# Transposing the rows of the second LayerNorm in blocks 0 to 2 with VectorE instead of TensorE

## The chip, the core and the metric

The kernel runs on one core of a Trainium2 chip. The core has five engines that each take their instructions in program order: TensorE (PE in the profile, with its weight loads shown apart as PEld), VectorE (DVE), ScalarE (ACT), GpSimd (POOL) and SyncE (SP), which here only issues DMAs. They wait for each other through semaphores. The metric is the device time of one launch in microseconds, the median of several runs.

## What is computed

One transformer block on 2048 rows of 512 elements, in float32: an attention with 32 heads of 16 that share one key and one value head, then a gated feed-forward layer with 1792 hidden elements.

```python
x = A_x
h = x + attention(layernorm(x), wq, wk, wv, wo)        # 32 heads, one k and one v
h2 = h + (gelu(layernorm(h) @ w_gate) * (layernorm(h) @ w_up)) @ w_down
return h2
```

The change concerns `layernorm(h)`, the second LayerNorm. Its rows must be turned, so that the 512 model elements stand on the partitions, before the products with `w_gate` and `w_up` can be taken.

## The kernel before

The 2048 rows are worked on in four blocks of 512, each of four tiles of 128 rows (`t` 0 to 3). Attention runs through all blocks as one long stream of scores: for each group of four heads and each chunk of 128 keys, TensorE makes two pairs of score tiles (`s`, L371), ScalarE takes the exponential of each pair (`p`, L375), and TensorE later weighs the values with them (`acc`, L379). One `s` move is a pair of matmuls and one exponential over 128x1024 elements.

The dense work of blocks 0 to 2 is woven into the attention of the blocks after them. It is a queue of products, made in this order for block `b`: four projections `pp_b_t` (the attention output times `wo`), two remaining products `pd` of block `b-1` with `w_down`, then `pg` and `pu` for each of the 14 chunks of the hidden elements (gate and up), with `pd` in between. All terms are split in a high and a low part, so a projection has 12 terms. Each product is made twice, on the upper and on the lower 64 rows of the array (`pp_b_t_0` and `pp_b_t_1` in the order of instructions), in two PSUM banks; VectorE adds both into an SBUF tile. One `d` move (`step`, L808) issues one matmul of the first half and, six moves behind (`LAG`), one of the second, which run beside each other. The halves take the three spare banks in turn, first in, first out.

The order of the stream is written out by hand. `CYCLES` (L47) lists rounds of `s` and `d` moves; each round begins with `finish`, which issues the value weighings of two or three chunks. A round is called idle when the queue cannot give enough `d` moves (`available`, L767): it then uses a second list with `s` and `v` (weighing) alone. A product may carry a condition; `pg_b_0`, the first of the gate products, may be started only when all four tiles of its block have been turned.

At the end of each half product and at the start of each round the program issues up to two steps of a side queue, `later` (`side`, L577). VectorE's and SyncE's instructions are in the order in which the program issues them, and no scheduler moves them; the same holds for TensorE, ScalarE and GpSimd.

For tile `t` the way from projection to turned rows is: `done` (L609 to L615) adds the two halves into `h`; `norm` takes mean and variance on VectorE (`bn_stats`, `bn_aggr`) and lets GpSimd make `rstd`; the step `scale` lets VectorE write the normalised rows over the input tile `xb` (L603). `before`, at the start of a round, calls `turn` once `SETTLE` = 14 moves have passed since then: four TensorE transposes into a spare PSUM bank (`pxt`, L624), from which VectorE makes the high part `x2h` (L629) and the low part `x2l` (L630). `turn` also issues the load of the input tile three ahead (`load_x`, L551); the pool `xb` has three buffers. The variable `clock` counts program moves, not time.

Of the kernel before, what the change touches and what calls it, by code (L numbers as in the profile page):

```python
# [9 lines left out]
F32 = mybir.dt.float32  # L10
# [4 lines left out]
ALU = mybir.AluOpType  # L15
# [4 lines left out]
P = 128  # L20
# [21 lines left out]

LAG = 6

SETTLE = 14

CYCLES = (  # L47
    (3, "ssdddddsdddsddds", "vssvssvs"),
# [11 lines left out]
def kernel(  # L60
# [12 lines left out]
    nc = tc.nc  # L73
    x = x.flatten_outer_dims()
# [8 lines left out]
    TB = T // P  # L83
    DC = D // P
# [19 lines left out]
    ident = const.tile([P, P], F32, name="ident")  # L104
# [54 lines left out]
    def run(outer, first):  # L159
# [304 lines left out]
        db = tiny = None  # L464
# [86 lines left out]
        def load_x(i):  # L551
            b, t = divmod(i, TB)
            if b == NB - 1:
                return
            xbs[b, t] = db.tile([P, D], F32, tag="xb", bufs=3, name=f"xb_{b}_{t}")
            nc.sync.dma_start(xbs[b, t], x_t[:, i, :])

        w1s, w2s, xbs, hs, xTs = {}, {}, {}, {}, {}
        scaled_at, halves, gs, gated = {}, {}, {}, set()
        tanhs, later = [], []  # L560
        clock = 0

        def new_xT(b):
            xTs[b] = [
                db.tile([P, DC, T], F32R, tag=f"x2{w[0]}", bufs=1, name=f"x2{w[0]}_{b}")
                for w in ("hi", "lo")
            ]

        def prime():
            new_xT(0)  # L570
            for i in range(3):
                load_x(i)
                load_w1(i)
            for j in range(3):
                load_w2(0, j)
# [13 lines left out]
        def project(b, t):  # L589
            def terms():  # L590
                o_hi, o_lo = o_blk[b]
                sl = slice(t * P, (t + 1) * P)
                return product_terms([
                    (None, (o_hi[:, c, sl], o_lo[:, c, sl]), (wo_hi[:, c, :], wo_lo[:, c, :]))
                    for c in range(DC)
                ])

            def norm():
                x = xbs[b, t]
                scaled = layer_norm(tiny, x, hs[b, t], f"2_{b}_{t}")  # L600

                def scale():
                    scaled()  # L603
                    scaled_at[b, t] = clock

                later.insert(min(1, len(later)), scale)

            def done(a, bank):
                if a == 0:  # L609
                    h = db.tile([P, D], F32, tag="h", bufs=6, name=f"h_{b}_{t}")  # L610
                    nc.vector.tensor_tensor(h, bank, xbs[b, t], op=ALU.add)
                    hs[b, t] = h
                else:
                    nc.vector.tensor_tensor(hs[b, t], hs[b, t], bank, op=ALU.add)
                    later.append(norm)  # L615

            return f"pp_{b}_{t}", 3 * DC, terms, done, lambda: pieces.get(b, 0) > t

        def turn(b, t):
            tag, bank = take_bank(f"pxt_{b}_{t}")  # L620
            pt = bank.rearrange("p (c q) -> p c q", c=DC)
            xn = xbs.pop((b, t))
            for c in range(DC):
                nc.tensor.transpose(pt[:, c, :], xn[:, c * P : (c + 1) * P], ident)  # L624
            if b not in xTs:
                new_xT(b)
            sl = slice(t * P, (t + 1) * P)
            hi, lo = (x[:, :, sl] for x in xTs[b])
            nc.vector.tensor_copy(hi, pt)  # L629
            nc.vector.tensor_tensor(lo, pt, hi.bitcast(F32), op=ALU.subtract)  # L630
            spare.append(tag)
            load_x(b * TB + t + 3)
            turned[b] = t + 1

        turned = {}

        def up(b, f, k):
            def terms():
                w = w1s.pop((b, f, k))
                hi, lo = xTs[b]  # L640
                return product_terms([
                    (None, (w[:, 0, c, :], w[:, 1, c, :]), (hi[:, c, :], lo[:, c, :]))
                    for c in range(DC)
                ])
# [12 lines left out]
            def done(a, bank):  # L657
                tag = "gu"[k]
                if a == 0:
                    half = db.tile([P, T], F32, tag=tag, bufs=2, name=f"{tag}_{b}_{f}")  # L660
                    nc.vector.tensor_copy(half, bank)  # L661
                    halves[b, f, k] = half
                else:
                    half = halves[b, f, k]
                    nc.vector.tensor_tensor(half, half, bank, op=ALU.add)  # L665
                    load_w1(b * 2 * FC + 2 * f + k + 3)
                    if k == 0:
                        later.extend((square, cube))
                    else:
                        later.append(lambda: tanhs.append((b, f)))  # L670

            ready = (lambda: turned.get(b, 0) == TB) if f == 0 and k == 0 else None
            return f"p{'gu'[k]}_{b}_{f}", 3 * DC, terms, done, ready

        def bend(b, f):
# [89 lines left out]
        queue, at, ahead = [], 0, 0  # L765
# [282 lines left out]
        with tc.manual_schedule(engines={mybir.EngineType.SP, mybir.EngineType.DVE}):  # L1048
            parts = None
            if first:  # L1050
                work = later_q()
                parts = part_weights(early.enter_context(tc.tile_pool(name="parts", bufs=1)))
# [60 lines left out]
        def before(idle):  # L1113
            if outs:
                take_out()
            while (b_t := divmod(sum(turned.values()), TB)) in scaled_at:
                if clock - scaled_at[b_t] < SETTLE:
                    break
                turn(*b_t)
                if not idle:  # L1120
                    break
            bent = list(tanhs)
            tanhs.clear()
            for key in bent:
                bend(*key)
            side(100 if idle else 2)
            return bent
# [8 lines left out]
        for i in range(-((lead - end) // 16)):  # L1136
            if first and i in BOUND_LISTS:
                bound_flag(BOUND_LISTS.index(i))
            for count, woven, plain in CYCLES:
                idle = available() < woven.count("d")  # L1140
# [410 lines left out]
```

## Time and profile before

| | |
|---|---|
| median of 3 runs | 1399.07 us |
| lowest and highest run | 1398.49, 1399.08 us |
| profiled execution, its span | 1401.0 us |
| TensorE busy | 1386.0 us (99%) |
| ScalarE busy | 1033.9 us (74%) |
| VectorE busy | 632.4 us (45%) |
| GpSimd busy | 233.8 us (17%) |
| TensorE transposes of the change (`pxt`, L624) | 48, first at 332.6 us, last at 984.7 us |

The span is that of one profiled execution, on whose clock all places in the trace are given. A busy share is an average over stages; for the woven stages, from about 320 us to 1260 us, what an instruction costs must be read from the stretch where it stands. The three groups of `pxt` stand at 332 to 349 us (block 0), 640 to 663 us (block 1) and 962 to 985 us (block 2).

### The profile page before, as it was taken

Reading aid. Unit: us, or ns where it says so; the run is one execution under the profiler, and the core shown is the slowest. Engines: PE = TensorE matmul, PEld = TensorE weight load, DVE = VectorE, ACT = ScalarE, POOL = GpSimd, SP = SyncE. Lnnn points to the kernel's source line nnn. Section 1 sums busy time; section 2 is a strip of 40 time slices with the busy share of each in tenths; the row PEclk is TensorE's granted clock in tenths of the full one; section 3 lists DMA queues with packets and bytes.
Section 4 is the critical chain, followed back from the end, with each engine's and each line's share of the span. In section 5 each row is a group of like instructions: output and inputs, shape, how many; then the busy total and the mean of one; then the engine's idle time right before and its main releaser. Section 6 shows DMA issues by size and latency. Waiting matters only on the chain.

```text
span 1401.0 us, 25275 instructions
## 1 busy us (share of the span) xinstructions
PE 1386.0 (99%) x10438; PEld 757.0 (54%) x10438; DVE 632.4 (45%) x1016; ACT 1033.9 (74%) x1157; POOL 233.8 (17%) x336
## 2 busy tenths in 40 slices
PE   9999999999999999999999999999999999999998
PEld 7433333325555555545555555545555555558886
DVE  7413131314354444455364444445264443546665
ACT  8799999997787777877787777777778777762000
POOL 7577766731000000000000000000000000011000
PEclk9999999999999999999999999999999999999999
DMA  4466776744232322311422323311322332233552
GB/s 162 159 208 199 237 225 207 229 171 157 79 104 75 117 103 103 118 58 58 169 92 80 133 103 102 107 61 43 141 98 103 118 103 102 97 117 121 188 207 94
DMA packets 66783, 180.32 MB, mean 129 GB/s; under 512 B 9672, under 2 KB 9672, under 8 KB 66628
## 3 DMA queue, kind: packets, MB, share of 16 engines
q1 hardware_dynamic: 55196, 143.15, 29.4%
q0 software_dynamic: 10208, 35.26, 7.7%
q8 instruction: 84, 1.38, 0.4%
q10 hardware_dynamic: 1256, 0.20, 0.1%
q14 instruction: 39, 0.32, 0.1%
HBM read 130.87 MB, written 47.45 MB: 127 GB/s over the span
## 4 chain that ended last, share of the span: by engine, by line
PE 82%; POOL 7%; DMA 5%; issue 2%; ACT 2%; DVE 1%; POOLq 0%; ACTq 0%
PE acc L379 27%; PE s L371 16%; PE pu L798 8%; PE pg L798 8%; PE pd L798 7%; DMA w_1r<-in_B_w_up_dram 4%; PE pd L828 3%; PE pg L828 3%; PE pu L828 3%; PE pp L798 2%; ACT p L375 1%; PE pq L220 1%; POOL w_1b L129 1%; PE pp L901 1%; PE pd_rest L840 1%
## 5 line engine op out<-in xcount | busy, mean ns | idle before, releaser
L375 ACT ACTIVATE p<-s 128x1024 f32<-128x1024 f32 x1024 | 959.5, 1037 | 226.4 <-PE s L371 223.7
L379 PE MATMUL acc<-p,v_sb 128*32 128x512 f32 x4096 | 491.0, 599 | 0.2 <-DVE oT L392 0.2
L371 PE MATMUL s<-qg,kaug 50*128 50x512 f32 x1984 | 387.0, 427 | 4.2 <-ACT p L375 4.1
L371 PEld LDWEIGHTS s<-qg,kaug 50*128 50x128 f32 x1984 | 168.9, 184 | 283.2 <-ACT p L375 124.4
L379 PEld LDWEIGHTS acc<-p,v_sb 128*32 128x32 f32 x4096 | 108.7, 109 | 233.3 <-issue 219.5
L798 PE MATMUL pg<-x2h,w 64*128 64x512 f32 x672 | 175.8, 392 | 0.0
L798 PE MATMUL pu<-x2h,w 64*128 64x512 f32 x672 | 174.3, 392 | 0.0
L798 PE MATMUL pd<-w,gh 64*128 64x512 f32 x624 | 122.7, 394 | 0.3
L728 DVE TENSOR_TENSOR h<-h,pd 128x512 f32<-128x512 f32 x80 | 54.9, 686 | 145.9 <-PE pd L798 145.9
L138 POOL TENSOR_SCALAR rstd<-mv 128x1 f32<-128x1 f32 x16 | 3.6, 224 | 670.5 <-DVE mv L136 670.2
L798 PEld LDWEIGHTS pg<-x2h,w 64*128 64x128 f32 x672 | 96.0, 186 | 11.1
L798 PEld LDWEIGHTS pu<-x2h,w 64*128 64x128 f32 x672 | 95.5, 186 | 11.1
L798 PE MATMUL pg<-x2l,w 64*128 64x512 f32 x336 | 100.4, 392 | 0.0
L798 PE MATMUL pu<-x2l,w 64*128 64x512 f32 x336 | 99.8, 392 | 0.0
L957 ACT ACTIVATE ga<-ga 128x512 f32<-128x512 f32 x14 | 8.8, 632 | 88.5 <-DVE ga L954 88.5
L798 PEld LDWEIGHTS pd<-w,gh 64*128 64x128 f32 x624 | 67.3, 186 | 12.6 <-DVE u L665 1.4
L392 DVE COPY oT<-acc 128x512 f32<-128x512 f32 x32 | 22.1, 690 | 110.0 <-PE acc L379 109.9
L798 PE MATMUL pd<-w,gl 64*128 64x512 f32 x312 | 70.6, 392 | 0.0
L665 DVE TENSOR_TENSOR g<-g,pg 128x512 f32<-128x512 f32 x42 | 28.8, 685 | 90.9 <-PE pg L798 90.9
L415 DVE RECIPROCAL oc<-oc 128x128 f32<-128x128 f32 x64 | 56.6, 922 | 21.4 <-DMA oc<-acc_d 17.5
L661 DVE COPY g<-pg 128x512 f32<-128x512 f32 x42 | 29.0, 692 | 72.1 <-PE pg L798 72.1
L665 DVE TENSOR_TENSOR u<-u,pu 128x512 f32<-128x512 f32 x42 | 28.8, 685 | 68.7 <-PE pu L798 68.7
(259 smaller groups left out, 1481.2 us busy)
## 6 DMA issues: line engine op xcount, KB each, us to landing
w<-w_d SPq DMA_DIRECT2D x126, 512.0 KB
w<-w_d SPq DMA_DIRECT2D x21, 1024.0 KB
qg<-q_d SPq DMA_DIRECT2D x62, 200.0 KB
q_d<-qh SPq DMA_DIRECT2D x32, 256.0 KB
acc_d<-oT SPq DMA_DIRECT2D x31, 256.0 KB
oc<-acc_d SPq DMA_DIRECT2D x124, 64.0 KB
w_d<-w_0b POOLq DMA_DIRECT2D x14, 512.0 KB, 3.8
w_d<-w_1b POOLq DMA_DIRECT2D x14, 512.0 KB, 5.1
```

Of the source, the lines that this page charges most:

```text
L129: (eng_lo or nc.vector).tensor_tensor(lo, src, hi.bitcast(F32), op=ALU.subtract)
L220: nc.tensor.matmul(pq, wt[c][:, d, :], xt[:, d, :], start=(n == 0), stop=(n == 3 * DC - 1),)
L371: nc.tensor.matmul(s[:, a, :], kaug[rows, kc * P : (kc + 1) * P], qg[rows, u, :], start=True, stop=True,)
L375: nc.scalar.activation(p[:, 2 * u : 2 * u + 2, :], s, AF.Exp, scale=SCALE)
L379: nc.tensor.matmul(acc[32 * j : 32 * j + 32, :], v_sb[:, kc, :], p[:, j, :], start=(kc == 0), stop=(kc == KC - 1), skip_group_check=True,)
L392: nc.vector.tensor_copy(oT, acc)
L415: nc.vector.reciprocal(oc[:, 1, sl], oc[:, 1, sl])
L661: nc.vector.tensor_copy(half, bank)
L665: nc.vector.tensor_tensor(half, half, bank, op=ALU.add)
L728: nc.vector.tensor_tensor(hs[b, t], hs[b, t], bank, op=ALU.add)
L798: nc.tensor.matmul(bank, lhsT[r], rhs[r], start=(k == 0), stop=(k == n - 1), skip_group_check=True,)
L828: nc.tensor.matmul(bank, lhsT, rhs, start=(i == 0), stop=(i == len(ts) - 1))
```

## The change

TensorE's 48 transposes and their PSUM bank go. `turn` now gives a list of five steps that `norm` puts into the side queue, behind the step that scales: four steps of four VectorE transposes each and a last one. One VectorE transpose reads 32 partitions of the normalised rows and writes 32 partitions of a new SBUF tile `raw`: four blocks of 32 by 32. Sixteen of them turn a tile. The last step issues the load of the input tile two ahead (no longer three), makes `x2h` and `x2l` from `raw`, and marks the tile as turned. `raw` comes from the pool `xb`, which still has three buffers, so only two input tiles are loaded at the start.

`SETTLE` is now 8 and has another place: `pg_b_0` may start 8 moves after the last tile's last step was issued. `before` no longer turns anything.

```diff
-SETTLE = 14
+SETTLE = 8
...
-                def scale():
-                    scaled()
-                    scaled_at[b, t] = clock
-
-                later.insert(min(1, len(later)), scale)
+                at = min(1, len(later))
+                later[at:at] = [scaled, *turn(b, t)]
...
         def turn(b, t):
-            tag, bank = take_bank(f"pxt_{b}_{t}")
-            pt = bank.rearrange("p (c q) -> p c q", c=DC)
             xn = xbs.pop((b, t))
-            for c in range(DC):
-                nc.tensor.transpose(pt[:, c, :], xn[:, c * P : (c + 1) * P], ident)
+            x = xn.rearrange("p (c k e) -> p c k e", c=DC, k=4)
...
-            hi, lo = (x[:, :, sl] for x in xTs[b])
-            nc.vector.tensor_copy(hi, pt)
-            nc.vector.tensor_tensor(lo, pt, hi.bitcast(F32), op=ALU.subtract)
-            spare.append(tag)
-            load_x(b * TB + t + 3)
-            turned[b] = t + 1
-
+            hi, lo = (w[:, :, sl] for w in xTs[b])
+            raw = db.tile([P, DC, P], F32, tag="xb", bufs=3, name=f"xt_{b}_{t}")
+
+            def blocks(k):
+                for i in range(4):
+                    nc.vector.transpose(
+                        raw[32 * k : 32 * k + 32, :, 32 * i : 32 * i + 32],
+                        x[32 * i : 32 * i + 32, :, k, :],
+                    )
+
+            def parts():
+                load_x(b * TB + t + 2)
+                nc.vector.tensor_copy(hi, raw)
+                nc.vector.tensor_tensor(lo, raw, hi.bitcast(F32), op=ALU.subtract)
+                turned[b] = t + 1
+                turned_at[b] = clock
+
+            return [*(partial(blocks, k) for k in range(4)), parts]
...
-            ready = (lambda: turned.get(b, 0) == TB) if f == 0 and k == 0 else None
+            ready = None
+            if f == 0 and k == 0:
+                ready = lambda: turned.get(b, 0) == TB and clock - turned_at[b] >= SETTLE
...
-            while (b_t := divmod(sum(turned.values()), TB)) in scaled_at:
-                if clock - scaled_at[b_t] < SETTLE:
-                    break
-                turn(*b_t)
-                if not idle:
-                    break
```

The order of instructions shows where the work now stands. First TensorE in block 0, behind the last projection. Before:

```order
L798 MATMUL pp_3_1_3652<-wo_hi,o_lo_1710 128x512
L624 MATMUL pxt_1_3690<-ident,xb_1_3261 128x128 x4
L624 MATMUL pxt_2_3699<-ident,xb_2_3265 128x128 x4
L379 MATMUL acc_1_3500<-p_3590,v_sb 32x512 x4
L371 MATMUL s_0_3713<-qg_1_3234,kaug 128x512 x2
L371 MATMUL s_1_3717<-qg_1_3234,kaug 128x512 x2
L379 MATMUL acc_1_3500<-p_3620,v_sb 32x512 x4
L371 MATMUL s_0_3726<-qg_1_3234,kaug 128x512 x2
L371 MATMUL s_1_3730<-qg_1_3234,kaug 128x512 x2
L379 MATMUL acc_1_3500<-p_3656,v_sb 32x512 x4
L371 MATMUL s_0_3739<-qg_1_3234,kaug 128x512 x2
L624 MATMUL pxt_3_3743<-ident,xb_3_3602 128x128 x4
```

Now, from the first score pair behind the last projection to the first gate product (the row of `pg_0_0` that reads `x2h`):

```order
L371 MATMUL s_0_3768<-qg_1_3234,kaug 128x512 x2
L371 MATMUL s_1_3772<-qg_1_3234,kaug 128x512 x2
L379 MATMUL acc_1_3499<-p_3643,v_sb 32x512 x4
L371 MATMUL s_0_3781<-qg_1_3234,kaug 128x512 x2
L371 MATMUL s_1_3785<-qg_1_3234,kaug 128x512 x2
L379 MATMUL acc_1_3499<-p_3679,v_sb 32x512 x4
L371 MATMUL s_0_3794<-qg_1_3234,kaug 128x512 x2
L379 MATMUL acc_1_3499<-p_3767,v_sb 32x512 x4
L379 MATMUL acc_1_3499<-p_3780,v_sb 32x512 x4
L371 MATMUL s_1_3806<-qg_1_3234,kaug 128x512 x2
L371 MATMUL s_0_3811<-qg_1_3234,kaug 128x512 x2
L808 MATMUL pg_0_0_3815<-x2h_3255,w_0_0_0_3259 128x512
```

Seven score pairs now stand between the last projection and the first gate product; before there were 13. One idle round of six score moves has gone from here. The number of idle rounds is the same, six: the second of block 0 now stands at the end of block 0's products instead, just ahead of the idle round that was there already. From the start of block 1's projections on, the rounds are the same as before.

Second, VectorE in block 0, from the last projection's second half (`h_3`) to the first copy of a gate product (`g_0`). Before:

```order
L614 TENSOR_TENSOR h_3_3672<-h_3_3672,pp_3_1_3652 128x512
L135 BN_STATS st_0_3_3682<-h_3_3672 128x6
L136 BN_AGGR mv_0_3_3683<-st_0_3_3682 128x2
L603 TENSOR_SCALAR xb_3_3602<-h_3_3672,mv_0_3_3683,rstd_0_3_3686 128x512
L629 CAST x2h_3255<-pxt_1_3690 128x4x128
L630 TENSOR_TENSOR x2l_3256<-pxt_1_3690,x2h_3255 128x4x128
L629 CAST x2h_3255<-pxt_2_3699 128x4x128
L630 TENSOR_TENSOR x2l_3256<-pxt_2_3699,x2h_3255 128x4x128
L629 CAST x2h_3255<-pxt_3_3743 128x4x128
L630 TENSOR_TENSOR x2l_3256<-pxt_3_3743,x2h_3255 128x4x128
L661 COPY g_0_3861<-pg_0_0_3808 128x512
```

Now:

```order
L612 TENSOR_TENSOR h_3_3695<-h_3_3695,pp_3_1_3675 128x512
L628 STREAM_TRANSPOSE xt_2_3704<-xb_2_3570 32x4x32 x16
L635 CAST x2h_3255<-xt_2_3704 128x4x128
L636 TENSOR_TENSOR x2l_3256<-xt_2_3704,x2h_3255 128x4x128
L135 BN_STATS st_0_3_3734<-h_3_3695 128x6
L136 BN_AGGR mv_0_3_3735<-st_0_3_3734 128x2
L580 TENSOR_SCALAR xb_3_3670<-h_3_3695,mv_0_3_3735,rstd_0_3_3738 128x512
L628 STREAM_TRANSPOSE xt_3_3741<-xb_3_3670 32x4x32 x16
L635 CAST x2h_3255<-xt_3_3741 128x4x128
L636 TENSOR_TENSOR x2l_3256<-xt_3_3741,x2h_3255 128x4x128
L669 COPY g_0_3847<-pg_0_0_3815 128x512
```

The statistics of tile 3 now stand behind the 16 transposes of tile 2, and another 16 follow before the last `x2l`. The 32 transposes of tiles 0 and 1 stand ahead of this piece, in groups of 8, 8, 12 and 4 between the additions of the projections.

Third, VectorE in block 1, around the addition of the first half of the last projection (`h_3` from `pp_3_0`). Before:

```order
L614 TENSOR_TENSOR h_2_6804<-h_2_6804,pp_2_1_6788 128x512
L135 BN_STATS st_1_2_6862<-h_2_6804 128x6
L136 BN_AGGR mv_1_2_6863<-st_1_2_6862 128x2
L603 TENSOR_SCALAR xb_2_3750<-h_2_6804,mv_1_2_6863,rstd_1_2_6866 128x512
L629 CAST x2h_6816<-pxt_1_6891 128x4x128
L630 TENSOR_TENSOR x2l_6817<-pxt_1_6891,x2h_6816 128x4x128
L392 COPY oT_0_6908<-acc_0_6466 128x512
L611 TENSOR_TENSOR h_3_6926<-pp_3_0_6843,xb_3_6820 128x512
```

Now, from the scaling of tile 1:

```order
L580 TENSOR_SCALAR xb_1_3759<-h_1_6781,mv_1_1_6845,rstd_1_1_6848 128x512
L628 STREAM_TRANSPOSE xt_1_6851<-xb_1_3759 32x4x32 x12
L612 TENSOR_TENSOR h_2_6873<-h_2_6873,pp_2_1_6857 128x512
L628 STREAM_TRANSPOSE xt_1_6851<-xb_1_3759 32x4x32 x4
L635 CAST x2h_6756<-xt_1_6851 128x4x128
L636 TENSOR_TENSOR x2l_6757<-xt_1_6851,x2h_6756 128x4x128
L135 BN_STATS st_1_2_6962<-h_2_6873 128x6
L136 BN_AGGR mv_1_2_6963<-st_1_2_6962 128x2
L580 TENSOR_SCALAR xb_2_6840<-h_2_6873,mv_1_2_6963,rstd_1_2_6966 128x512
L392 COPY oT_0_6979<-acc_0_6548 128x512
L609 TENSOR_TENSOR h_3_6997<-pp_3_0_6914,xb_3_6937 128x512
```

Ahead of this addition there are now 32 transposes, 16 of tile 0 and 16 of tile 1, which were not on VectorE before. Block 2 has the same order as block 1. On SyncE the loads of the input tiles stand where the last steps of `turn` now are; everything else keeps its order but for the shift by one round in block 0.

More of the change, by code (lines that the diff above doesn't have):

```diff
@@ L558, in run @@
         w1s, w2s, xbs, hs, xTs = {}, {}, {}, {}, {}
-        scaled_at, halves, gs, gated = {}, {}, {}, set()
+        halves, gs, gated = {}, {}, set()
         tanhs, later = [], []
@@ L571, in prime @@
             for i in range(3):
-                load_x(i)
+                if i < 2:
+                    load_x(i)
                 load_w1(i)
@@ L627, in turn @@
             sl = slice(t * P, (t + 1) * P)
-            hi, lo = (x[:, :, sl] for x in xTs[b])
-            nc.vector.tensor_copy(hi, pt)
-            nc.vector.tensor_tensor(lo, pt, hi.bitcast(F32), op=ALU.subtract)
-            spare.append(tag)
-            load_x(b * TB + t + 3)
-            turned[b] = t + 1
+            hi, lo = (w[:, :, sl] for w in xTs[b])
[13 more added lines that the diff above has]
+            return [*(partial(blocks, k) for k in range(4)), parts]
+        turned_at = {}
         turned = {}
```

## The prediction

> **What bounds the kernel.** I read the page first, then the busy times by stretch (columns: busy us and instructions of PE, PEld, DVE, ACT and POOL, then granted TensorE clock, DMA share and GB/s).
>
> ```profile
> span 1401.0 us, 25275 instructions
> PE 82%; POOL 7%; DMA 5%; issue 2%; ACT 2%; DVE 1%; POOLq 0%; ACTq 0%
> ```
> ```profile
> 353.80:595.00 241.20, 241.20 (x2016) 133.99 (x2018) 113.67 (x178) 186.70 (x206) 0.00 (x0) 1.00 0.29 100
> 286.10:289.40 3.30, 3.30 (x18) 0.91 (x20) 0.00 (x0) 2.87 (x4) 2.26 (x3) 0.50 0.72 240
> 615.20:620.60 5.40, 5.04 (x37) 1.41 (x35) 4.11 (x10) 4.98 (x6) 0.00 (x0) 1.00 0.46 146
> ```
>
> TensorE carries 82% of the chain that ended last. In the woven stage (first stretch) it is never idle, VectorE is busy 47% of the time and ScalarE 77%. So TensorE time taken out there comes off the end, and a TensorE wait put in there is added to it. Only an idle round (last stretch) goes at ScalarE's pace: five exponentials, 4.98 of 5.40 us.
>
> **What the removed transposes cost.** The timeline of TensorE (start, length, engine, line, operation) shows an ordinary passage from scores to weighings, then one with a turn in block 1, then two in block 0:
>
> ```profile
> 325.16 0.40 PE L371 MATMUL s<-qg,kaug 50*128 50x512 f32 x2
> 325.50 1.92 PE L379 MATMUL acc<-p,v_sb 128*32 128x512 f32 x16
> 327.91 0.40 PE L798 MATMUL pp<-wo_lo,o_hi 64*128 64x512 f32 x2
> ...
> 331.86 0.43 PE L371 MATMUL s<-qg,kaug 50*128 50x512 f32 x2
> 332.56 0.63 PE L624 MATMUL pxt<-ident,xb 128*128 128x128 f32 x4 [0.28 <-DMA oc<-acc_d]
> 333.12 2.78 PE L379 MATMUL acc<-p,v_sb 128*32 128x512 f32 x24
> ...
> 341.02 0.39 PE L798 MATMUL pp<-wo_hi,o_lo 64*128 64x512 f32 x1
> 341.34 1.41 PE L624 MATMUL pxt<-ident,xb 128*128 128x128 f32 x8
> 342.68 1.06 PE L379 MATMUL acc<-p,v_sb 128*32 128x512 f32 x8
> ...
> 640.30 0.40 PE L371 MATMUL s<-qg,kaug 50*128 50x512 f32 x2
> 641.22 2.78 PE L379 MATMUL acc<-p,v_sb 128*32 128x512 f32 x24
> ```
>
> Without a turn, the passage takes 325.50 - 325.16 = 0.34 us. With one it takes 0.92 (640.30 to 641.22), so a turn costs 0.58; blocks 1 and 2 have eight, 4.6 us. In block 0 the first costs 1.26 - 0.34 = 0.9 and the next two together 1.66 - 0.34 = 1.3 us. The fourth lies in an idle round, where ScalarE sets the pace: nothing. Sum of the gain: **6.9 us**.
>
> **The moved round.** An idle round of six scores goes from the start of block 0 to its end, beside the one there. As many idle rounds of the same lengths remain, in two runs as before: nothing. But it was cover. It ran while VectorE finished the turned rows; now the first `pg` stands six scores earlier in TensorE's order. `SETTLE` counts program moves, so it holds back no instruction on the chip.
>
> **VectorE in block 0.** All 64 transposes of the block stand on one in-order engine, ahead of the last `x2l`, which the second matmul of `pg_0_0` reads. The trace has no such instruction. The nearest rows are a tile's pieces, float32 with the same 128 elements per partition from SBUF to SBUF (timeline of VectorE):
>
> ```profile
> 617.84 0.29 DVE L432 TENSOR_TENSOR oc<-oc 128x128 f32<-128x128 f32 x1
> 618.16 0.23 DVE L128 CAST o_hi<-oc 128x128 fp32r<-128x128 f32 x1
> 618.42 0.29 DVE L129 TENSOR_TENSOR o_lo<-oc,o_hi 128x128 fp32r<-128x128 f32 x1
> 618.63 0.95 DVE L415 RECIPROCAL oc<-oc 128x128 f32<-128x128 f32 x1
> ```
>
> A follower that needs the result starts 0.32 us after (617.84 to 618.16), one that doesn't 0.21 us after (618.42 to 618.63); the slowest operation of the size lasts 0.95. Near ends are thus 0.21 and, should a block be filled and emptied one after the other, about 0.45 (my estimate: 0.32 plus another 128 elements at the 0.23 of the CAST, less overlap). I take **0.32**, because no row of a turned block can leave before the block is in, so overlap with the next is unlikely.
>
> [...]
>
> The rest of the list comes from the groups (busy us, mean ns, idle before) and two rows of the timeline:
>
> ```profile
> L392 DVE COPY oT<-acc 128x512 f32<-128x512 f32 x32 | 22.1, 690 | 110.0 <-PE acc L379 109.9
> L695 DVE CAST gh<-ga 128x512 fp32r<-128x512 f32 x42 | 17.5, 416 | 0.3
> L135 DVE BATCH_NORM_STATS2 st<-h 128x6 f32<-128x512 f32 x12 | 8.3, 695 | 0.4
> L630 DVE TENSOR_TENSOR x2l<-pxt,x2h 128x512 fp32r<-128x512 f32 x12 | 8.3, 691 | 0.4
> L614 DVE TENSOR_TENSOR h<-h,pp 128x512 f32<-128x512 f32 x12 | 8.2, 687 | 20.1 <-PE pp L798 20.0
> L603 DVE TENSOR_SCALAR xb<-h,mv,rstd 128x512 f32<-128x512 f32 x12 | 6.6, 546 | 12.0 <-POOL rstd L139 12.0
> L136 DVE BATCH_NORM_AGGREGATE mv<-st 128x2 f32<-128x6 f32 x16 | 2.9, 182 | 0.5
> ```
> ```profile
> 326.85 0.55 DVE L603 TENSOR_SCALAR xb<-h,mv,rstd 128x512 f32<-128x512 f32 x1 [1.02 <-POOL rstd L139]
> ...
> 349.53 0.69 DVE L630 TENSOR_TENSOR x2l<-pxt,x2h 128x512 fp32r<-128x512 f32 x1
> ```
>
> From the first scaling (326.85) on: four scalings 2.2; six additions and one `oT` copy 4.8; three times statistics 2.6; four times `x2h` (now from SBUF, so the 0.42 of L695 for L629's PSUM read) and `x2l` 4.4; three waits of 1.0 for `rstd`, of which one addition hides 0.7, 2.3. That is 16.3 us. The input tile of `t`+2 is now requested only after the transposes of `t`. A load's way I take from two rows of SyncE, a store of the same 256 KB and the load that waits for it:
>
> ```profile
> 328.20 0.33 SPq L444 DMA_DIRECT2D acc_d<-oT  x1
> 330.28 1.72 SPq L410 DMA_DIRECT2D oc<-acc_d  x4
> ```
>
> 2.1 us, against the 1.1 of `x2h` and `x2l` beside it: the last projection waits 1.0 more, and tile 2's (behind those `oc` loads on SyncE) about 0.3. Two loads of block 1's tiles now hold SyncE until tiles 2 and 3 are turned; the query tiles of the next group stand ahead of them, and the weights behind them are asked for only once `pg_0_0` is done, so that costs nothing. So the rows are complete at 326.85 + 16.3 + 1.3 + 64 x 0.32 = **364.9**, against 350.2 before.
>
> TensorE arrives earlier. Weighings began at 342.68; less 2.2 us of turns, 340.5; one idle round, 5.4; two weighings and two score pairs, 2.4 (325.50 to 327.91): the first `pg` at 348.3, and its second matmul 0.2 later. Before it was here:
>
> ```profile
> 353.76 2.78 PE L379 MATMUL acc<-p,v_sb 128*32 128x512 f32 x24
> 356.47 0.73 PE L371 MATMUL s<-qg,kaug 50*128 50x512 f32 x4
> 357.04 0.39 PE L798 MATMUL pg<-x2h,w 64*128 64x512 f32 x1
> ```
>
> 6.8 us after the last `x2l`. So TensorE now waits 364.9 - 348.5 = **16.4 us**. Behind the waiting matmul stand the scores, so ScalarE runs dry after the two score buffers, and nothing makes the time up.
>
> A wait has a second price. The stretch 286.1 to 289.4 above ran at a granted clock of 0.50; the trace shows it behind a few waits of TensorE for ScalarE. A 3.3 us stretch at half clock costs **1.7 us**, which I add once, for the long wait.
>
> [...]
>
> **Blocks 1 and 2.** Two `pd` products stand between the projections and `pg`, so the rows come in time. But VectorE also empties the three banks:
>
> ```profile
> 634.42 0.55 DVE L603 TENSOR_SCALAR xb<-h,mv,rstd 128x512 f32<-128x512 f32 x1 [1.01 <-POOL rstd L139]
> ...
> 651.39 0.68 DVE L611 TENSOR_TENSOR h<-pp,xb 128x512 f32<-128x512 f32 x1
> ...
> 653.00 0.69 DVE L614 TENSOR_TENSOR h<-h,pp 128x512 f32<-128x512 f32 x1 [0.93 <-PE pp L798]
> ```
>
> The second half of the first `pd` starts when the last projection's second half ends (653.0, less 0.2 of array latency: 652.8) and takes the bank emptied at 651.39 to 652.07. Two turns less, it would start at 651.6. Now, from 634.42 to the end of that addition: 32 transposes 10.2, and scalings, additions, `oT`, statistics, parts and two `rstd` waits 10.8: 655.4. TensorE waits **3.8 us**, 7.6 in both blocks. The `oT` copy, 4 us late, delays the next weighing (653.9) less than that same wait does.
>
> Sum: -6.9 + 16.4 + 1.7 + 7.6 = **+18.8 us**. The profiled execution lies 1.9 us above the median; I apply the change to the median, 1399.1 + 18.8 = **1417.9**.
>
> **Rivals.** *Quick transposes:* at 0.21 they finish in block 0 about 6.7 us earlier (a wait of 9.7), and 3.5 earlier in the others (0.3 each): -6.9 + 9.7 + 1.7 + 0.6 = +5.1, 1404. For it: the 0.21 row; against it: a block must fill. *Faster, the other side:* VectorE keeps up, and only the gain remains, 1392. Slope and waits give equality at 0.14 to 0.15 per transpose, and faster by 0.2% needs 0.11 or less. For it: VectorE idle half the time; against it: the shortest row above, six elements, lasts 0.18, and 128 elements lasted 0.23 or more. *Slow transposes:* at 0.45, 8.1 us more in block 0 and 4.2 in each other: 1434. That the transposes stay on TensorE is excluded by the order.
>
> **How the numbers follow.** Forecast 1417.9 (0.26 to 0.40 per transpose, 1410 to 1428): 0.62. Quick, 1402 to 1410: 0.16. Slow, above 1428: 0.09. Between 0.11 and 0.18, within 0.2% of before (about what a measurement of this kernel can tell from no change): 0.06. Faster: 0.07. So slower 0.87, same 0.06, faster 0.07. The range 1402 to 1430 leaves out the faster, the same and most slow cases, 2 in 10.
>
> **What would show it.** A transpose's mean and its step in the timeline (0.32); no `pxt`, and 0.34 us passages in their place; `pg_0_0` held in block 0 by `x2l`, with ScalarE idle, about 16 us, and a low clock behind it; a wait of 4 us at the first `pd` in blocks 1 and 2, ended by `h<-pp,xb`; two idle rounds side by side at block 0's end. The forecast is wrong if VectorE's transposes overlap, if the first `pg` isn't held, or if the banks are free in time.

## The result and the profile after

| | before | after |
|---|---|---|
| median of five runs | 1399.07 us | 1425.58 us |
| lowest and highest run | 1398.49, 1399.19 us | 1421.78, 1428.21 us |
| ratio to before, 95% interval | | 1.0188, 1.0177 to 1.0199 |
| profiled execution, its span | 1401.0 us | 1420.1 us |

The kernel is 26.5 us slower. The profiled execution after the change is the fastest of its five (1421.78 us). Its mean granted clock is 0.991; the other four have 0.988, and that will matter below.

The head of the page of the kernel after, and the shares of its chain of waits:

```profile
span 1420.1 us, 25369 instructions
PE 88%; DVE 5%; ACT 2%; issue 2%; DMA 2%; POOL 1%; DVEq 0%; ACTq 0%; POOLq 0%
```

VectorE had 1% of the chain and now has 5%: where TensorE waits, the chain runs back through VectorE's list. TensorE's waits in the kernel after (engine and line, what it waited for, total us, times, longest):

```profile
PE pg L808 <- issue: 14.8, 1, 14.8
PE pd L808 <- DVE h L609: 6.6, 2, 3.3
...
PE pp L911 <- DVE oT L392: 1.3, 1, 1.3
PE pp L808 <- DVE h L609: 0.8, 1, 0.8
```

One wait at the first `pg` of block 0, two at a `pd` in blocks 1 and 2, and two small ones that I had not forecast. "issue" for the first means that the profile names no releaser. The timeline of VectorE in block 0 names it. The first rows show the start of its list, the last two the end:

```profile
324.61 0.55 DVE L580 TENSOR_SCALAR xb<-h,mv,rstd 128x512 f32<-128x512 f32 x1 [1.02 <-POOL rstd L139]
325.19 2.50 DVE L628 STREAM_TRANSPOSE xt<-xb 32x128 f32<-32x128 f32 x8
327.73 0.69 DVE L392 COPY oT<-acc 128x512 f32<-128x512 f32 x1
328.45 0.69 DVE L609 TENSOR_TENSOR h<-pp,xb 128x512 f32<-128x512 f32 x1
...
335.01 0.69 DVE L609 TENSOR_TENSOR h<-pp,xb 128x512 f32<-128x512 f32 x1 [0.70 <-DMA xb<-in_A_x_dram]
...
344.54 0.69 DVE L609 TENSOR_TENSOR h<-pp,xb 128x512 f32<-128x512 f32 x1 [1.41 <-DMA xb<-in_A_x_dram]
...
361.81 0.43 DVE L635 CAST x2h<-xt 128x512 fp32r<-128x512 f32 x1
362.27 0.69 DVE L636 TENSOR_TENSOR x2l<-xt,x2h 128x512 fp32r<-128x512 f32 x1
```

TensorE in the same place:

```profile
329.20 0.50 PE L808 MATMUL pp<-wo_hi,o_hi 64*128 64x512 f32 x1 [0.81 <-DVE h L609]
...
346.84 0.73 PE L371 MATMUL s<-qg,kaug 50*128 50x512 f32 x4
362.34 0.76 PE L808 MATMUL pg<-x2h,w 64*128 64x512 f32 x1 [14.77 <-issue]
363.02 0.79 PE L808 MATMUL pg<-x2l,w 64*128 64x512 f32 x1
```

The first `pg` starts 0.10 us after the last `x2h` ends (361.81 + 0.43), the second 0.06 us after the last `x2l` (362.27 + 0.69). So the wait is for VectorE's list. ScalarE stands still with it: its next exponential starts after 16.24 us.

```profile
365.56 1.02 ACT L375 ACTIVATE p<-s 128x1024 f32<-128x1024 f32 x1 [16.24 <-PE s L371]
```

The stretches around the wait (us, then busy us and instructions of PE, PEld, DVE, ACT and POOL, granted clock, DMA share, GB/s):

```profile
347.57:362.34 14.77, 0.01 (x3) 0.03 (x1) 13.16 (x41) 1.75 (x2) 1.45 (x3) 0.62 0.08 18
362.34:368.19 5.85, 5.85 (x23) 4.34 (x24) 0.62 (x1) 1.88 (x2) 0.00 (x0) 0.50 0.14 45
```

TensorE works again at 362.34, but at half clock for another 5.85 us. If all of it went at half pace, 2.9 us would be lost; a run below measures 2.3.

### The profile page after: what moved, and what is told of

It reads as the page before. It is cut to its first block, busy times and chain, and to the rows that moved or that the text cites. A ratio compares the mean times of both kernels' runs of the same rounds, so it can differ in the third digit from the quotient of the medians.

```text
span 1420.1 us, 25369 instructions
## 1 busy us (share of the span) xinstructions
PE 1382.1 (97%) x10390; PEld 749.7 (53%) x10390; DVE 688.3 (48%) x1208; ACT 1035.1 (73%) x1157; POOL 231.2 (16%) x336
## 4 chain that ended last, share of the span: by engine, by line
PE 88%; DVE 5%; ACT 2%; issue 2%; DMA 2%; POOL 1%; DVEq 0%; ACTq 0%; POOLq 0%
PE acc L379 31%; PE s L371 19%; PE pg L808 8%; PE pu L808 8%; PE pd L808 6%; PE pq L220 3%; PE pd L838 3%; PE pg L838 3%; PE pu L838 3%; DVE xt L628 2%; ACT p L375 2%; PE pp L808 1%; PE pp L911 1%; PE pd_rest L850 1%; DMA xb<-in_A_x_dram 1%
## 5 line engine op out<-in xcount | busy, mean ns | idle before, releaser
L371 PEld LDWEIGHTS s<-qg,kaug 50*128 50x128 f32 x1984 | 172.0, 184 | 286.3 <-ACT p L375 133.7
L808 PE MATMUL pg<-x2h,w 64*128 64x512 f32 x672 | 175.1, 396 | 14.8 <-issue 14.8
L808 PE MATMUL pu<-x2h,w 64*128 64x512 f32 x672 | 170.8, 391 | 0.0
L808 PEld LDWEIGHTS pg<-x2h,w 64*128 64x128 f32 x672 | 96.3, 188 | 27.1 <-issue 15.2
L415 DVE RECIPROCAL oc<-oc 128x128 f32<-128x128 f32 x64 | 56.6, 921 | 27.5 <-DMA oc<-acc_d 23.6
L628 DVE STREAM_TRANSPOSE xt<-xb 32x128 f32<-32x128 f32 x192 | 58.1, 303 | 2.8
```

Source lines behind the costliest of these rows:

```text
L371: nc.tensor.matmul(s[:, a, :], kaug[rows, kc * P : (kc + 1) * P], qg[rows, u, :], start=True, stop=True,)
L415: nc.vector.reciprocal(oc[:, 1, sl], oc[:, 1, sl])
L628: nc.vector.transpose(raw[32 * k : 32 * k + 32, :, 32 * i : 32 * i + 32], x[32 * i : 32 * i + 32, :, k, :],)
L808: nc.tensor.matmul(bank, lhsT[r], rhs[r], start=(k == 0), stop=(k == n - 1), skip_group_check=True,)
```

## The experiments

Two theories stood against each other. **Mine:** the loss is the sum of three waits at places that can be named, most of it in block 0, and of the half clock behind them; the transposes as such cost TensorE nothing. **The rival:** the loss is spread, because VectorE carries 58 us more and everything that waits for VectorE gets later, in all blocks alike. Ratios below are to the kernel before, run on the same chip.

### One block at a time

In two kernels VectorE turns only some of the blocks; TensorE's `turn` comes back for the others, as `turn_pe`, with its wait of 14 moves:

```
-                later[at:at] = [scaled, *turn(b, t)]
+                later[at:at] = [scale] if b in ON_PE else [scaled, *turn(b, t)]
...
+            while (b_t := divmod(sum(turned.values()), TB)) in scaled_at:
+                if clock - scaled_at[b_t] < 14:
+                    break
+                turn_pe(*b_t)
```

With `ON_PE = (0,)`:

> Block 0 is turned by TensorE as before the change (wait of 14 moves, loads three tiles ahead), blocks 1 and 2 by VectorE as after it. Theory (the loss sits in block 0: the wait of 14.8 us at the first pg, and the clock behind it): only the two bank waits of 3.3 us, the gain of 4.6 us from eight removed turns and at most one half-clock stretch are left, so 1399 to 1406 us. Rival (the loss is spread over the blocks, or comes from VectorE's work as such): two thirds of the 26.5 us are left, about 1417 us.

Measured: 1407.03 us, ratio 1.0043 (1.0027 to 1.006), so 6.0 us of the 26.5 are left, within what my theory expected as a ratio and far from the rival's 1417. With `ON_PE = (1, 2)`:

> Block 0 is turned by VectorE as after the change, blocks 1 and 2 by TensorE as before it. Theory: block 0's loss of about 17 to 22 us is all there, so 1416 to 1422 us, with a wait of about 15 us at the first pg. Rival (spread loss): a third of the 26.5 us, about 1408 us.

Measured: 1418.72 us, ratio 1.0126 (1.0109 to 1.0143), that is 17.6 us. The two losses add up to 23.6 of 26.5 us. TensorE's waits, of the first kernel (one row) and of the second (two):

```profile
PE pd L834 <- DVE h L616: 6.5, 2, 3.3
```
```profile
PE pg L837 <- issue: 14.9, 1, 14.9
...
PE pp L837 <- DVE h L617: 0.8, 1, 0.8
```

Each kernel has the waits of its own blocks, of the same lengths as after the change. The only other one that the change brought is 0.6 us for an `oT` copy behind the woven stage, in the first kernel. The loss belongs to the places, not to VectorE's load.

### The idle round as cover

`SETTLE` is a number for each block now; in block 0 it is 18, then 36:

```
-SETTLE = 8
+SETTLE = (18, 8, 8)
...
-                ready = lambda: turned.get(b, 0) == TB and clock - turned_at[b] >= SETTLE
+                ready = lambda: turned.get(b, 0) == TB and clock - turned_at[b] >= SETTLE[b]
```

> As after the change, but the idle round stands at the start of block 0 again (block 0 waits 18 moves behind its last turned tile, the others 8). Theory: the first pg is asked for one idle round (5.4 us) later while VectorE finishes at the same moment, so the wait falls from 14.8 to about 9.4 us and the time by 5.4 us or a little more (less half clock): 1417 to 1420 us; one idle round alone at the end of block 0. Rival (the wait isn't set by the moment VectorE finishes, but moves along with TensorE, for example by ScalarE's or the loads' pace): the wait stays near 15 us and the time near 1425 us.

Measured: 1419.84 us, ratio 1.0128 (1.0111 to 1.0145).

> As after the change, but block 0 waits 36 moves behind its last turned tile, so that three idle rounds stand ahead of its first pg (two more than after the change) and none at its end. Theory (the wait ends when VectorE has the rows; an idle round is 5.4 us in which TensorE's other work goes on): the wait falls from 14.8 by two rounds to 3 to 4 us, the half-clock stretch behind it to 3.4 to 6.8 us, and the time to 1410 to 1414 us. Rival (idle rounds cost what they cover): no lower than the kernel with one idle round moved back, 1420 us.

Measured: 1412.19 us, ratio 1.0095 (1.0078 to 1.0112). The waits at the first `pg`, of one round back and of two more:

```profile
PE pg L808 <- issue: 8.7, 1, 8.7
```
```profile
PE pg L808 <- issue: 3.3, 1, 3.3
```

From 14.8 to 8.7 to 3.3: each round of scores takes 5.4 to 6.1 us off the wait, and the moment at which VectorE has the rows stays: the first `pg` starts 37.7 us behind the block's first scaling in the kernel after, and 38.1 us behind it in both of these. An idle round was cover, as the prediction says, and more of it costs little: it is the same scores, done earlier. The first of these kernels gains only 0.2 us in its profiled execution (span 1419.9 us, clock 0.989 against 0.991), although the wait is 6.1 us shorter, mainly because it has more half clock: from 285.82 to 289.23, where the kernel after has none (1.00 from 282.85 to 289.67); 6.91 us behind the first wait, where the kernel after has 5.85; and at both bank waits, where the kernel after has it at block 2's alone. The stretches at the bank waits (columns as above):

```profile
664.70:671.52 6.82, 5.52 (x27) 3.46 (x31) 6.57 (x20) 2.84 (x3) 0.00 (x0) 0.50 0.32 109
992.38:995.79 3.41, 3.41 (x21) 2.23 (x20) 3.24 (x11) 2.05 (x2) 0.00 (x0) 0.50 0.27 87
```

### The clock by itself

Transposes of the identity are added ahead of block 0's first `pg`, into the bank that `pg` then overwrites. They change no result; they only keep TensorE busy.

```
                 r = slice(64 * a, 64 * a + 64)
+                if a == 0 and name == "pg_0_0":
+                    for _ in range(100):
+                        nc.tensor.transpose(bank[:, :P], ident, ident)
```

> As after the change, with 100 transposes of the identity added on TensorE ahead of the first pg of block 0, into the bank that pg then overwrites; at 0.13 us each (16 of L882 in 2.1 us) they fill 13 of the 14.8 us in which TensorE waits. Theory (the clock is a price of its own): the granted clock stays at 1.0 in and behind the wait, and the time falls by 2.9 us (the profiled execution) to 7 us (what lies between the profiled execution and the median): 1418 to 1423 us. Rival (the clock costs nothing beside the wait): the same time as after the change, 1425.6 us, or longer.

Measured: 1425.89 us, ratio 1.0179 (1.0162 to 1.0196): no gain. The timeline of TensorE shows why:

```profile
347.44 11.14 PE L805 MATMUL pg<-ident 128*128 128x128 f32 x100
362.57 0.76 PE L811 MATMUL pg<-x2h,w 64*128 64x512 f32 x1 [3.99 <-issue]
```

The 100 transposes took 11.14 us, not 13, and left 3.99 us idle, and the half clock came all the same: the `pg` matmul lasts 0.76 us here too. With `range(132)`:

> As after the change, with 132 added transposes of the identity ahead of the first pg of block 0 in place of 100: at the 0.111 us each that the run with 100 showed (11.14 us) they last 14.7 us and leave less than a microsecond of the wait idle, where 100 left 4.0 us, with a half clock from 361.53 to 368.35 all the same. [...] Rival (what the slower start costs is made up by other work): no difference from 1425.9 us.

My estimate was that 2.9 us would go, half of the 5.85 us at half clock. Measured: 1423.24 us, ratio 1.0173 (1.0156 to 1.019). The two ratios cannot be told apart by their intervals, so the runs leave the size open. The trace doesn't. The same two rows with 132 transposes, and the first weighing behind them, then that weighing with 100:

```profile
362.52 0.47 PE L811 MATMUL pg<-x2h,w 64*128 64x512 f32 x1 [0.64 <-issue]
...
367.38 2.78 PE L379 MATMUL acc<-p,v_sb 128*32 128x512 f32 x24
```
```profile
369.71 2.78 PE L379 MATMUL acc<-p,v_sb 128*32 128x512 f32 x24
```

From the same start (362.52 and 362.57) the next weighing comes 2.28 us earlier (4.86 against 7.14 us). So the half clock behind this wait costs 2.3 us up to that weighing. In the profiled executions of both these kernels the bank waits of both blocks have half clock behind them, one stretch more than in the kernel after (with 100, 672.14 to 675.55 in block 1; the mean clocks are 0.994 and 0.996).

### The loads

The turned blocks go to buffers that are free at that time, the tags `g` and `u`, so the input tiles can be loaded three ahead again:

```
-            raw = db.tile([P, DC, P], F32, tag="xb", bufs=3, name=f"xt_{b}_{t}")
+            raw = db.tile([P, T], F32, tag="gu"[t % 2], bufs=2, name=f"xt_{b}_{t}")
+            raw = raw.rearrange("p (c q) -> p c q", c=DC)
...
-                load_x(b * TB + t + 2)
+                load_x(b * TB + t + 3)
```

> As after the change, but the input tiles are loaded three ahead as before it, because the turned blocks go to the free buffers of the gate halves (tags g and u) and not to an input tile's. Theory: in block 0 VectorE's waits for the loads (0.70 and 1.41 us in the profiled execution) go, so the rows are complete some 2 us earlier, and in block 1 a wait of 0.28; the first pg's wait falls to about 12.7 us and the time by 2 to 3 us, to 1423 us. Rival (VectorE then waits for rstd or for TensorE at the same places): less than 0.5 us.

Measured: 1421.99 us, ratio 1.0162 (1.0145 to 1.0179), 3.6 us less than after the change; the intervals overlap by a little. The wait at `pg` is 13.0 us. What VectorE's instructions on `h` waited for in block 0, behind the first scaling, in the kernel after and in this one (us, times):

```profile
  DMA xb<-in_A_x_dram: 2.1, 2
  POOL rstd L139: 2.0, 2
```
```profile
  POOL rstd L139: 2.4, 3
```

The 2.1 us for the loads are gone, and 0.4 us of waiting for `rstd` came in their place: 1.7 us, as the wait at `pg` shows (14.8 to 13.0). The other half of the 3.6 us has no name in the trace; the intervals allow for it.

### The pace of the transposes

Each transpose is split in two of 64 elements with the same groups of partitions:

```
+                    for c in (slice(0, 2), slice(2, 4)):
                         nc.vector.transpose(
-                            raw[32 * k : 32 * k + 32, :, 32 * i : 32 * i + 32],
-                            x[32 * i : 32 * i + 32, :, k, :],
+                            raw[32 * k : 32 * k + 32, c, 32 * i : 32 * i + 32],
+                            x[32 * i : 32 * i + 32, c, k, :],
```

> As after the change, with each transpose split in two of 64 elements per partition, with the same groups of 32 partitions in and out for both, so that only every second one goes to another group. By the step of 0.315 us for 128 elements and 1.04 ns an element (0.29 us for 128 and 0.69 us for 512 elements of TENSOR_TENSOR), a half that waits for the one before takes 0.25 us. Theory (the groups keep a follower from overlapping): the second of a pair follows after 0.07 to 0.15 us, so a pair lasts about 0.4, a tile 6.2 to 6.4 us against 5.05, and block 0's wait is 5 us longer. Rival (every transpose waits for the one before, whatever its groups): a pair lasts 0.5, a tile 8 us, and block 0's wait is 12 us longer.

Measured: 1434.66 us, ratio 1.0232 (1.0216 to 1.0247), the `pg` wait 18.1 us. Its transposes as a group (ns: shortest, median, longest), and three rows of VectorE's timeline from narrow windows: the first transpose, the second with the third, the third with the fourth.

```profile
L629 DVE STREAM_TRANSPOSE xt<-xb x384: 190/212/243, 325.9 to 1023.0; 32x64 f32<-32x64 f32 x192
```

```profile
325.95 0.23 DVE L629 STREAM_TRANSPOSE xt<-xb 32x64 f32<-32x64 f32 x1
```
```profile
326.12 0.44 DVE L629 STREAM_TRANSPOSE xt<-xb 32x64 f32<-32x64 f32 x2
```
```profile
326.32 0.36 DVE L629 STREAM_TRANSPOSE xt<-xb 32x64 f32<-32x64 f32 x2
```

The second starts 0.17 us after the first, which lasts 0.23: it overlaps. The third, which reads another group of partitions, starts 0.20 us after the second (326.32 - 326.12), and no transpose lasts less than 0.19: it begins when the second is over. All 192 pairs do the same: the second starts 0.16 to 0.17 us after the first, and none that goes to another group starts before the one ahead of it has ended. A tile takes 6.00 us against 5.05:

```profile
350.66 6.00 DVE L629 STREAM_TRANSPOSE xt<-xb 32x64 f32<-32x64 f32 x32
```

So my theory stands, but not all of its numbers: a pair lasts 0.37 us (about 0.4 expected) and a tile 6.00 (6.2 to 6.4), while the second of a pair follows later than the 0.07 to 0.15 us that I had. The `pg` wait grows by 3.3 us and not by 5; the time grows by about 6 us by the ratios, as the waits at `pd` grow too, from 6.6 to 10.2 us in all. So the step of 0.32 us goes with the change of the group: in the kernel after, where every transpose reads another group than the one ahead of it, 16 take 5.05 us, 0.315 each; here the second of a pair follows after 0.16 to 0.17 us and only the next one, in another group, waits for the end.

### Taking the bank wait away

Block 0 is turned by TensorE. In blocks 1 and 2 the steps of tiles 1 and 2 are held back in a list until the first addition of tile 3 has been issued; loads and buffers are those of the loads' experiment:

```
+                    if t == TB - 1:
+                        later.extend(held)
+                        held.clear()
...
+                if b not in ON_PE:
+                    rest = later if t in (0, TB - 1) else held
+                    at = at + 1 if t == 0 else len(rest)
+                    rest[at:at] = turn(b, t)
```

> Block 0 is turned by TensorE; in blocks 1 and 2 VectorE turns tile 0 at once but tiles 1 and 2 only behind the first addition of tile 3 (which empties the bank that the first pd waits for), with loads three ahead and the turned blocks in the gate halves' buffers; an idle round stands ahead of the first pg of blocks 1 and 2, in place of two idle rounds later. Theory (the bank wait is an effect of order): both waits of 3.3 us go, with the half-clock stretches behind them, and the gain of 4.6 us from the eight turns is left: 1394.5 to 1398 us. Rival (VectorE is full from 650 to 686, so the wait only moves to the first pg or to the next bank): 3 us or more of wait in each block, 1401 us or more.

Measured: 1402.5 us, ratio 1.003 (1.0017 to 1.0043), a miss: the time is the rival's, but not by its mechanism. The waits in blocks 1 and 2 are gone from the trace, so they are an effect of order, as I held (in the loads' experiment, with the same loads and buffers, they stood at 6.6 us). But a new wait stands at the end of the woven stage:

```profile
1250.13 1.22 PE L842 MATMUL pd<-w,gh 64*128 64x512 f32 x4 [3.08 <-DVE h L772]
```

The idle rounds ahead of `pg` pulled scores forward, so `pd` products were left behind the last of them, one after the other, and there they wait for a bank, with 3.06 us at half clock behind the wait. Of the 4.6 us gained, 3.1 and about 1.5 went there, which makes it as long as before; the 4 us by the ratio (3.2 between the medians) are not explained.

The last kernel avoids both. VectorE turns only tiles 0 and 3 of blocks 1 and 2; nothing is held back, and the idle rounds are those of the kernel before:

```
+ON_DVE = {(1, 0), (1, 3), (2, 0), (2, 3)}
...
+                later[at:at] = [scaled, *turn(b, t)] if (b, t) in ON_DVE else [scale]
```

> VectorE turns only tiles 0 and 3 of blocks 1 and 2, TensorE the other eight tiles as before the change; loads three ahead, the turned blocks in the gate halves' buffers, idle rounds where they stood before the change. Theory (a bank wait comes when 32 transposes stand ahead of the last tile's first addition; 16 are 5.05 us less than that, more than the wait of 3.3): no wait at pd or pg, and the gain of four removed turns of 0.58 us is left: 1396 to 1398 us where before gives 1399.3. Rival (any transposes ahead of an addition delay the banks): a wait of 1 us or more in each block, 1399 us or more.

Measured: 1398.29 us against 1401.0 us of the kernel before on that chip, ratio 0.998 (0.9971 to 0.9989): 2.8 us faster by the ratio (1.5 to 4.1), against 2.3 forecast. In the trace the weighings behind the four removed turns come 0.58 to 0.59 us earlier each, 2.3 in all. TensorE waits for VectorE at none of the places named here, and no half clock stands in the woven stages (the mean clock is 0.999). The head of its page:

```profile
span 1394.5 us, 25308 instructions
...
PE 1380.6 (99%) x10422; PEld 750.0 (54%) x10422; DVE 650.8 (47%) x1080; ACT 1033.6 (74%) x1157; POOL 231.5 (17%) x336
```

This version is faster than both kernels, than the one before by 0.2%. Its span is not to be set against the 1401.0 us of before, whose profiled execution holds a half-clock stretch (286.1 us) and lies above its own median. With 16 transposes ahead of the last addition instead of 32, the banks come in time.

## Why the prediction was right, and where it was off

The forecast was 1417.9 us, the range 1402 to 1430, the sign slower; the time is 1425.6. The mechanism was right at every named place; the clock acted at one place more than the sum charged. The sum was 7.7 us short. Of that, 2.0 us show in the profiled executions (20.8 us between them, worked out below, against 18.8 forecast). The other 5.7 are 3.8 by which the median after lies above its profiled execution (1425.58 against 1421.78) and 1.9 by which the median before (1399.07) lies below its own, taken without half clock (a span of 1399.3, and 1.7 for the launch around it as in 1421.78 against 1420.1).

**The pace, 0.32 us per transpose.** Measured by the group row and by 16 in 5.05 us, 0.315:

```profile
L628 DVE STREAM_TRANSPOSE xt<-xb 32x128 f32<-32x128 f32 x192 | 58.1, 303 | 2.8
```

The reason given (a block must be in before it leaves) is too simple: the split transposes overlap where the groups stay. So the number was right partly by luck: the second of a pair starts 0.16 to 0.17 us into the first, which lasts 0.19 us or more; only where the group changes, as it does at every step of the kernel after, is there no overlap. (The rivals' products are slightly off: 64 x 0.11 is 7.0 us, not 6.7, and 64 x 0.13 is 8.3, not 8.1. Neither moves a forecast by more than half a microsecond.)

**VectorE's list in block 0.** Forecast from the first scaling to the complete rows: 364.9 - 326.85 = 38.05 us. Measured: 362.96 - 324.61 = 38.35. The loads' share was 1.3 and is 2.1 (0.70 + 1.41).

**The wait, 16.4 us.** It is 14.77 up to the first matmul, which reads `x2h`. Up to the end of `x2l`, as the prediction counts it, it is 15.2 (362.96 - 347.57, less 0.2 for that matmul). TensorE came 1.5 us later than I had it (347.57 - 324.61 = 22.96 us behind the first scaling, against 348.3 - 326.85 = 21.45). Of these, 0.81 is a wait that I missed: in block 0, too, the second half of a projection needs the bank that the addition at 328.45 empties, which stands behind eight transposes and the `oT` copy. This wait, ahead of the larger one, costs nothing more, since VectorE ends at the same moment; only the split between the two was off.

**The bank waits, 3.8 us each.** As waits they are 3.28 and 3.27, ended by the addition I had named:

```profile
670.12 0.50 PE L808 MATMUL pd<-w,gh 64*128 64x512 f32 x1 [3.28 <-DVE h L609]
```
```profile
992.77 0.77 PE L808 MATMUL pd<-w,gh 64*128 64x512 f32 x1 [3.27 <-DVE h L609]
```

What they cost in time can be read between the starts of the weighings ahead of and behind them. In block 1 it was 7.32 us before, with a turn of 0.58 in it (648.50 to 655.82), and is 10.49 now (662.17 to 672.66): 3.75 us more without the turn, which is the forecast. In block 2, where half clock follows, it was 7.31 (970.41 to 977.72) and is 12.04 (984.82 to 996.86): 5.31 us. So that half-clock stretch costs 1.6 us.

**The gain, 6.9 us.** It is in the trace. Where a turn stood ahead of the weighing at 641.22, the same weighing now follows its score after 0.34 us:

```profile
655.13 0.41 PE L371 MATMUL s<-qg,kaug 50*128 50x512 f32 x2
655.47 1.07 PE L379 MATMUL acc<-p,v_sb 128*32 128x512 f32 x8
```

At all eight turns of blocks 1 and 2 TensorE gets ahead by 0.58 to 0.59 us, and in block 0 by 0.9 and 1.3, as forecast.

**The moved round, nothing.** As cover it was worth what the prediction says (5.4 forecast, 6.1 less wait with it back). Whether its new place costs something by itself was not tried. It may: from the weighing at 325.50 to the one at 641.22 (323.25 and 655.47 in the kernel after) TensorE takes 16.5 us longer, 17.1 without the first turn of block 1 in it, while block 0's terms make 15.7 (-2.2 + 14.8 + 0.8 + 2.3).

**The clock, 1.7 us: the term that was mis-sized.** "I add once, for the long wait", said the prediction, for a stretch of 3.3 us. In the profiled execution the half clock lasts 5.85 us behind the long wait and costs 2.3, and another 3.41 us behind block 2's bank wait cost 1.6: 3.9 us. The sum charged no half clock for the bank waits. In the trace block 2's had half clock behind it (0.50 from 992.83 to 996.24); block 1's, as long, kept the full clock (1.00 in the stretches of the last section).

The other four executions have a mean clock of 0.988 instead of 0.991. If all of that were TensorE work at half pace, 0.003 of 1424 us would be 4.3 us more, about the 3.8 us between the profiled execution and the median. This is not shown: there is no trace of those four, and the same working fails for the kernel with the round back, where 0.989 against 0.993 and 0.994 would make 6 us and the executions lie 3.3 us apart.

The sum by terms, with the gain as forecast and the rest as measured: -6.9 + 14.8 + 0.8 + 7.5 (twice 3.75) + 3.9 + 1.3 (a wait for `oT` behind the woven stage, which other runs show at 0 to 1.3 us) = +21.4 us for the profiled execution. The profiled execution of before, without the 1.7 us of its own half clock, has a span of 1399.3; 1420.1 - 1399.3 = 20.8. The two agree to 0.6 us, but only in sum: block 0 took 1.4 us more than its terms, and the rest 2.0 less. What makes the 5.7 us between the profiled executions and the medians is not shown.

## What to carry to other kernels

Work taken off the bounding engine is a gain only where the engine that takes it over has room *at that place*: 47% busy on average was no room in the 38 us between the block's first scaling and the first product that needs its rows, and none ahead of an addition that empties a bank. Move only as much as fits between the instructions that others wait for; a third of this change is a gain of 0.2%, all of it a loss of 1.9%. And price an added wait of 3 us on TensorE at up to twice its length, since one or two stretches at half clock may stand behind it: here 3.3 us of wait cost 3.8, 5.3 or 6.2.

## What the runs showed of the hardware

The half-clock stretches of these traces have a length in common. In the kernel after they run from 351.12 to 368.19 (17.07 us, five times 3.413) and from 992.83 to 996.24 (3.41); in the kernel before from 286.07 to 289.48 (3.41); with the round back, the one that begins at 664.70 lasts 6.82 us, twice as long. Their beginnings lie whole multiples of it apart: 641.71 us in the kernel after, 188.0 times 3.413; 310.61 us with 100 added transposes (361.53 and 672.14), 91.0 times; with the round back they begin at 357.50, 664.70 and 992.38, which is 90.0 and 96.0 times 3.413 apart. So within each of these traces they fall on a grid of 3.413 us. The bank waits of blocks 1 and 2 have the same length, but not the same place on it; the grid's stretches in which they lie (columns as above):

```profile
665.15:668.56 3.41, 1.70 (x15) 0.98 (x11) 2.31 (x6) 2.27 (x3) 0.79 (x2) 1.00 0.27 77
668.56:671.97 3.41, 1.85 (x16) 1.53 (x17) 3.33 (x10) 1.02 (x2) 0.00 (x0) 1.00 0.21 77
989.41:992.82 3.41, 0.14 (x3) 0.05 (x2) 2.38 (x6) 0.66 (x1) 0.79 (x2) 1.00 0.17 61
992.83:996.24 3.41, 3.41 (x16) 2.75 (x18) 3.24 (x11) 1.55 (x2) 0.00 (x0) 0.50 0.39 124
```

Block 1's wait is split evenly, TensorE works 1.70 and 1.85 us in the two stretches, and the clock stays. Block 2's all but fills one stretch (0.14 us of work), and the next runs at half clock. The stretch ahead need not be that empty: in the kernel with 100 added transposes it holds 1.35 us of work, and the next runs at half clock as well.

```profile
668.73:672.14 3.41, 1.35 (x12) 1.13 (x14) 3.09 (x8) 0.51 (x1) 0.23 (x1) 1.00 0.23 82
672.14:675.55 3.41, 3.41 (x19) 1.62 (x19) 3.24 (x11) 2.56 (x3) 0.00 (x0) 0.50 0.30 82
```

So in the stretches shown here 0.14 and 1.35 us of work were followed by half clock, and 1.70 and 1.85 were not; no stretch shown here lies between. The full clock does not come back with the first work. In the kernel after, the stretch in which the long wait ends (361.36 to 364.77, clock 0.50) holds 2.43 us of work, and the next one (364.77 to 368.18) still ran at 0.50, with TensorE busy throughout; the one after it ran at 1.00. The stretch ahead of 286.07 in the profiled execution of before is unlike the others: TensorE worked 2.28 us in it, more than in those that kept the clock, and the next ran at 0.50. With the same 2.28 us at the same place in the kernel after (282.85 to 286.26) the clock stayed at 1.00. So TensorE's busy time alone does not decide; why stays open.

```profile
282.66:286.07 3.41, 2.28 (x18) 0.86 (x10) 0.00 (x0) 3.22 (x4) 2.59 (x5) 1.00 0.68 225
```

Beside its 3.8 us a wait of the same 3.3 us cost nothing more (block 1 above), 1.6 us (block 2 above) or 2.5 us (the 6.82 us at half clock in block 1 of the kernel with the round back: 12.53 us from weighing to weighing, and the second one lasts 0.45 us longer). The five runs after the change lie 6.4 us apart and those before 0.7; such differences in half clock may be the reason, which is not shown.
